# Stacking a head's state and v to 128 stationary rows in a linear-attention and MoE kernel

## The chip, the cores and the metric

The kernel runs on one core of a Trainium2 chip. The metric is the time of one execution on the device, in microseconds. Three executions of the kernel before took 352.67, 353.18 and 351.98 us: a median of 352.67 us.

A core has five engines with an instruction line of their own: PE (TensorE: matmuls, whose weight loads the profile shows as PEld), DVE (VectorE), ACT (ScalarE), POOL (GpSimd) and SP (SyncE, which here issues the DMAs). Each works through its line in the order in which the program wrote it, and waits at an instruction whose inputs are not there yet.

## The reference

```python
def _attn_ref(r, k, v, w, u):              # 4 batches, 8 heads, 768 tokens, 48 dims a head, f32
    for t in range(S):
        kt, vt, rt = (k[:, :, t], v[:, :, t], r[:, :, t])
        cur = np.einsum('bhd,bhe->bhde', u[None] * kt, vt)
        y[:, :, t] = np.einsum('bhd,bhde->bhe', rt, state + cur)
        state = w[None, :, :, None] * state + np.einsum('bhd,bhe->bhde', kt, vt)

def _moe_ref(x, w_in, w_spatial, b_spatial, w_out):   # x: y, heads side by side, (4, 768, 384)
    h = np.maximum(x @ w_in, 0.0)                     # 384 -> 1024
    u, v = (h[..., :d_ff // 2], h[..., d_ff // 2:])
    v_n = (v - mean(v)) / np.sqrt(var(v) + 1e-06)
    v_s = np.einsum('ts,bsd->btd', w_spatial, v_n) + b_spatial[None, :, None]
    return (u * v_s) @ w_out                          # 512 -> 384
```

A linear attention with a decaying state of 48 x 48 a head comes first, and its output y is the input x of a gated MoE block with a spatial matmul over the 768 tokens.

## The kernel before

The tokens of each of the 4 batches are cut into 6 chunks of 128, so there are 24 chunks `m`; `c = m % 6` is the chunk's place in its batch. A chunk is done in two halves of 64 tokens (`z`), and the 8 heads in 4 pairs (`p`). For each chunk stand, in this order of dependence:

- `prep` (L421 to L444): two loads, `rk` (r and k with the dims on partitions) and `rkv` (r, k and v with the tokens on partitions). r and k are scaled by powers of the decay (by DVE and POOL), and POOL builds the tile `a`, whose diagonal is the u term.
- `scores` (L455, called S below): 16 matmuls of 64 x 64 into the PSUM tile `ps`. `products` (L471, P): 16 matmuls k^T v into the same tile, 8 in a batch's last chunk. Both use PE as four tiles of 64 x 64.
- `state` (L485 to L502): a predicated copy on DVE puts the masked scores into `a` (L485); DVE adds the products to the state (`t1`, then `s`, L496 to L502); ACT writes the state of both halves into the block tiles `sblk` (L478 and L479).
- `apply` (L516, A): y of the chunk, into the PSUM tile `xp`. For each half, 12 matmuls multiply scaled r by the state block and 12 multiply `a` by v: 48 in a chunk, 36 in the first chunk of a batch, which has no state for `z == 0`. Each has 128 contraction rows, 32 stationary columns and 64 moving columns, and writes 32 of the 128 output rows. `tile_position=(0, 32 * g)` puts it into one of four strips of 32 columns of PE. The 96 outputs of a head pair are three thirds of 32; the strips `g < 3` take third `g` of the pairs 0 to 2, strip 3 takes the three thirds of pair 3.
- `fin` (L550): xp is split into a rounded part and a rest, the tile `x`.

The MoE part multiplies in the rounded format fp32r three times over (high by high, high by low, low by high: L556, L557, L558), with 384 or 512 moving columns: `moe_v`, `moe_u`, `moe_sp`, `moe_out`. The weights w_in and w_out come as f64 and are taken apart on DVE, ACT and PE (L355 to L378) in the first part of the run; w_sp is split too (`ws_h`, `ws_l`).

The order of every engine's instructions is made when the program is built, by the planner `Plan`: each task has one or more `ways` (an engine, a cost), the planner runs a list schedule over them with its own costs and due times, and the instructions are written in that order. `BIAS` adds to the end time that the planner sees for an engine, so that it chooses another where there is a choice. `SLOTS` gives the number of buffers of each tile; `ps` and `xp` have one each.

Of the kernel before, what the change touches and what calls it, by code (L numbers as in the profile page):

```python
# [7 lines left out]
F32 = mybir.dt.float32  # L8
# [23 lines left out]
OK, OV = DM, DM + DM + 16  # L32
VB = 2 * D
ROW = OV + 2 * NP * VB
# [3 lines left out]
BIAS = 3  # L38
MOST_IN, MOST_OUT = 2, 1


class Task:
    def __init__(self, ways, lag, nominal, nbytes):
        self.ways, self.lag, self.nominal, self.nbytes = ways, lag, nominal, nbytes
        self.cost = min(w[1] for w in ways)
        self.before, self.after, self.bufs = set(), set(), []
        self.due = self.end = self.most = None
# [20 lines left out]
class Plan:  # L68
# [11 lines left out]
    def add(self, ways, r=(), w=(), lag=0.1, nominal=None, nbytes=0):  # L80
        t = Task(ways, lag, nominal, nbytes)
# [46 lines left out]

    def run(self):
# [6 lines left out]
        while ready:  # L136
            best = {}
            for t in ready:
# [4 lines left out]
                if t.nbytes and len(landed) >= self.LANES:  # L143
                    can = max(can, landed[-self.LANES])
                end, e, at = min((max(can, free.get(e, 1.0)) + c + (BIAS if e == "DVE" else 0), e, max(can, free.get(e, 1.0)))
                                 for e, c, *_ in t.ways)
                late = at <= free.get(e, 1.0) + 0.02
                key = (0, t.due, t.place) if late else (1, at, t.due, t.place)
                if e not in best or key < best[e][0]:
                    best[e] = (key, at, t)  # L150
            if not best:
                raise ValueError(f"no slot for any of {len(ready)} ready tasks")
            _, at, t, e = min(((x[0], x[1], x[2], e) for e, x in best.items()), key=lambda x: (x[1], x[2].due))
# [4 lines left out]
            _, cost, emit, two = next(w for w in t.ways if w[0] == e)  # L158
            if two and e == "DVE":
                cost += sum(max(0.0, min(y, at + cost) - max(x, at)) for x, y in shared[-3:])  # L160
            if two and e == "POOL":
                shared.append((at, at + cost))
# [6 lines left out]
            if t.nbytes:  # L169
                line = max(line, at + 1.2)  # L170
                slow = min(t.nbytes / self.SLOW, max(0.0, 5.2 - line))
                line += slow + (t.nbytes - slow * self.SLOW) / self.RATE
                t.end = line + self.FIRST_BYTE
# [11 lines left out]
            emit()  # L185
# [4 lines left out]
def fused_kernel(ctx, tc, rkT, rkvN, wT, uB, w_in, w_sp, b_sp, w_out, out):  # L190
# [4 lines left out]
    EARLY, STATS = 7, 1  # L195
# [3 lines left out]
    SLOTS = dict(rk=3, rkv=3, vn=6, gt=5, u=8, vs=4, g=2, ob=2, pm=4, ps=1, xp=1, x=2, s=2, t1=1, dg=2, q=2)  # L199
# [42 lines left out]
    def load(key, shape, dtype, src, nbytes, view=None, due=None):  # L242
# [3 lines left out]
        plan.add([("SP", 0.45, f, False)], (), [key], lag=0, nbytes=nbytes).most = due  # L246
# [586 lines left out]
```

## Time and profile before

| what | value |
|---|---|
| median of three executions | 352.67 us |
| profiled execution | 352.11 us |
| its span | 350.4 us |
| instructions in the span | 11537 |
| PE busy | 329.4 us |
| DVE, ACT, POOL busy | 171.2, 148.6, 225.3 us |
| apply (L516), from its first matmul to the scores after it, a chunk with a state (at 94.91 us) | 1.48 us |
| HBM read and written | 39.32 MB, 4.72 MB |

The span runs from the first to the last instruction of the core; the execution's own time is longer by what lies around it. In the page's rows a group has its line, engine, operation, `out<-in` by the program's tile names, shapes and count, then busy time, mean duration, and the idle time just ahead of it with what ended it. Rows in order of time begin with the start and the duration in microseconds. A plain f32 matmul leaves two records in the trace, an fp32r matmul one. The granted clock of TensorE was 1.00 in this execution.

### The profile page before, as it was taken

The numbers are of one execution on the slowest core, as the hardware profiler recorded it, in microseconds if no ns is written. First come the engines' busy times: TensorE is split into PE (matmuls) and PEld (weight loads), VectorE is DVE, ScalarE is ACT, GpSimd is POOL, SyncE is SP. The second block draws the span as 40 slices with busy tenths as digits, with TensorE's granted clock in tenths as the row PEclk, the third lists the DMA queues.
The fourth block names the chain that finished last, engine by engine and source line by source line (L and its number), as shares of the span: only waits on it lengthen the run. The fifth ranks groups of instructions, "written<-read, shape, count | busy, mean of one in ns | idle before, by whom it ended". The sixth has DMA issues, their size and how long they took to land.

```text
span 350.4 us, 11537 instructions
## 1 busy us (share of the span) xinstructions
PE 329.4 (94%) x5092; PEld 302.1 (86%) x5092; DVE 171.2 (49%) x353; ACT 148.6 (42%) x334; POOL 225.3 (64%) x215
## 2 busy tenths in 40 slices
PE   2876999899999999999999999999999999999994
PEld 1454678799999899999999899999999899999993
DVE  5598964878634555554233664454233343011030
ACT  4237867772333384641323374640323363611121
POOL 4888989999858765587855767486855240436310
PEclk9999999999999999999999999999999999999999
DMA  7999457762061344442153144342050000010101
GB/s 236 421 408 341 160 177 249 250 227 89 0 199 44 134 153 153 146 129 101 22 199 115 40 152 153 144 137 96 19 203 2 2 2 2 22 47 0 45 24 67
DMA packets 13153, 44.78 MB, mean 128 GB/s; under 512 B 1584, under 2 KB 4784, under 8 KB 13104
## 3 DMA queue, kind: packets, MB, share of 16 engines
q1 hardware_dynamic: 13104, 44.05, 35.4%
q8 instruction: 40, 0.66, 0.8%
q14 instruction: 9, 0.07, 0.1%
HBM read 39.32 MB, written 4.72 MB: 126 GB/s over the span
## 4 chain that ended last, share of the span: by engine, by line
PE 88%; DVE 6%; DMA 2%; issue 2%; ACT 1%; SPq 0%; DVEq 0%; ACTq 0%
PE pm L556 24%; PE pm L557 23%; PE pm L558 23%; PE xp L516 9%; PE ps L455 4%; PE ps L471 3%; DMA vn<-w_in 1%; PE pm L367 1%; DVE a L485 1%; DVE pm L355 1%; DVE vn L357 1%; DVE pm L359 1%; DVE rk L430 1%; DMA out<-ob 1%; DVE wi_l L378 1%
## 5 line engine op out<-in xcount | busy, mean ns | idle before, releaser
L556 PE MATMUL pm<-ws_h,vn 128*128 128x384 f32 x192 | 65.2, 340 | 0.0
L558 PE MATMUL pm<-ws_h,vn 128*128 128x384 f32 x192 | 64.7, 337 | 0.0
L557 PE MATMUL pm<-ws_l,vn 128*128 128x384 f32 x192 | 64.5, 336 | 0.0
L682 DVE TENSOR_TENSOR g<-pm,bb 128x384 f32<-128x384 f32 x32 | 17.8, 556 | 66.6 <-PE pm L558 62.7
L437 POOL TENSOR_TENSOR rkv<-rkv 128x384 f32<-128x384 f32 x24 | 26.3, 1096 | 37.2 <-DMA rkv<-rkvN 37.2
L229 POOL TENSOR_TENSOR vn<-vs,vn 128x512 fp32r<-128x512 f32 x24 | 32.6, 1378 | 27.2 <-ACT vn L233 14.8
L233 ACT CAST gt<-g 128x384 fp32r<-128x384 f32 x32 | 16.4, 514 | 72.6 <-POOL g L229 66.4
L229 POOL TENSOR_TENSOR g<-g,u 128x384 f32<-128x384 f32 x30 | 31.4, 1047 | 19.1 <-DVE g L682 19.1
L434 DVE TENSOR_TENSOR rk<-rk,tt 128x1024 f32<-128x1024 f32 x17 | 29.5, 1734 | 25.9 <-DMA rk<-rkT 25.9
L229 POOL TENSOR_TENSOR gt<-g,gt 128x384 fp32r<-128x384 f32 x30 | 30.5, 1016 | 15.0 <-ACT gt L233 15.0
L556 PEld LDWEIGHTS pm<-ws_h,vn 128*128 128x128 f32 x192 | 36.0, 188 | 0.3
L557 PEld LDWEIGHTS pm<-ws_l,vn 128*128 128x128 f32 x192 | 36.1, 188 | 0.0
L558 PEld LDWEIGHTS pm<-ws_h,vn 128*128 128x128 f32 x192 | 36.0, 188 | 0.0
L556 PE MATMUL pm<-wo_h,gt 128*128 128x384 f32 x96 | 32.9, 342 | 0.0
L556 PE MATMUL pm<-x,wi_h 128*128 128x384 f32 x93 | 32.5, 349 | 0.0
L558 PE MATMUL pm<-wo_h,gt 128*128 128x384 f32 x96 | 32.4, 338 | 0.0
L557 PE MATMUL pm<-wo_l,gt 128*128 128x384 f32 x96 | 32.4, 338 | 0.0
L557 PE MATMUL pm<-x,wi_h 128*128 128x384 f32 x93 | 31.4, 338 | 0.9 <-issue 0.9
L442 POOL TENSOR_TENSOR a<-diag,dg 128x512 f32<-128x512 f32 x24 | 26.1, 1086 | 8.2 <-PE xp L516 4.9
L558 PE MATMUL pm<-x,wi_l 128*128 128x384 f32 x93 | 31.3, 337 | 0.0
L485 DVE COPY_PREDICATED a<-mask,ps 128x512 f32<-128x512 uint32 x24 | 18.0, 751 | 25.8 <-PE ps L471 22.5
L441 POOL TENSOR_TENSOR rkv<-rkv,tn 128x384 f32<-128x384 f32 x24 | 30.2, 1260 | 0.0
(119 smaller groups left out, 701.4 us busy)
## 6 DMA issues: line engine op xcount, KB each, us to landing
rkv<-rkvN SPq DMA_DIRECT2D x24, 776.0 KB, 4.6
rk<-rkT SPq DMA_DIRECT2D x24, 512.0 KB, 6.0
out<-ob SPq DMA_DIRECT2D x24, 192.0 KB, 1.9
vn<-w_in SPq DMA_DIRECT2D x6, 512.0 KB, 10.2
gt<-w_sp SPq DMA_DIRECT2D x6, 384.0 KB, 10.5
gt<-w_out SPq DMA_DIRECT2D x4, 384.0 KB, 3.8
bb<-b_sp SPq DMA_DIRECT2D x1, 384.0 KB, 9.3
ub<-uB SPq DMA_DIRECT2D x1, 192.0 KB, 7.3
```

The costliest lines, as they stand in the source:

```text
L229: plan.add([(e, cost[e], lambda e=e: engine[e].tensor_tensor(**f()), True) for e in ways.split()], r, w)
L233: emit = dict(DVE=lambda: nc.vector.tensor_copy(**f()), ACT=lambda: nc.scalar.copy(f()["out"], f()["in_"]))
L434: dve(1024, lambda: nc.vector.tensor_tensor(out=rk(), in0=rk(), in1=tt.unsqueeze(1).to_broadcast([P, 2, NP, C]), op=ALU.mult), [RK, *TT], ...
L437: pool(DM, lambda: nc.gpsimd.tensor_tensor(out=n_(), in0=n_(), in1=k0(), op=ALU.mult), [RV], [rn])
L441: pool(DM, lambda: nc.gpsimd.tensor_tensor(out=k0(), in0=k0(), in1=tn_f, op=ALU.mult), [RV, rn, *TN], [kn])
L442: pool(512, lambda: nc.gpsimd.tensor_tensor(out=a.rearrange("s b q z t -> s (b q z) t"), in0=diag.unsqueeze(1).to_broadcast([P, H, HC]), i ...
L485: dve(512, lambda: nc.vector.copy_predicated(out=atiles[m % 2].rearrange("s b q z t -> s (b q) (z t)"), mask=mask_u.rearrange("s z t -> s ...
L516: nc.tensor.matmul(xp[32 * g:32 * g + 32, z, jt * HC:(jt + 1) * HC], lhsT, rhs, start=(z, g) not in began, stop=True, skip_group_check=Tru ...
L556: nc.tensor.matmul(o, lh, rh, start=first, stop=False)
L557: nc.tensor.matmul(o, lh, rl, start=False, stop=False)
L558: nc.tensor.matmul(o, ll, rh, start=False, stop=last)
L682: dve(384, lambda: nc.vector.tensor_tensor(out=g(), in0=T[PM][:, 0:TH], in1=bb[:, ts_], op=ALU.add), [PM, ("c", "bb")], [G])
```

## The change

Each head's state and v now stand on top of each other in one tile `sv` of 128 stationary rows (a head's state on the 64 rows of one half of the partitions, its v on the other half), and its scaled r and `a` in one tile `A` of 128 moving rows. So one matmul adds r by state and a by v, for one head `h` of the pair. A third of a pair's outputs that lies within one head takes one matmul, the third that straddles both takes two (`if k != 2 - 2 * h` leaves out the others): 32 a chunk, at a batch's first chunk as well, where the state rows are set to zero.

With it go: v is loaded apart from r and k, by two DMAs into `sv`; the rows of r and a that belong on other partitions are moved by `move`, which the planner gives to SP (a DMA from SBUF to SBUF) or to ACT (a copy); the state is written by four ACT copies instead of two; products takes 48 stationary columns instead of 64; the planner has a bias against ACT too; and `ps` becomes a fixed tile. The MoE part's own work is the same.

```diff
-BIAS = 3
+BIAS = dict(DVE=3.0, ACT=3.5)
...
+    sv = [const.tile([P, 2, 2, NP, HC], F32, name=f"sv{n}") for n in range(NV)]
+    pst = psum.tile([P, 2, 512], F32, name="ps")
...
-        load(("rkv", m), [P, ROW], F32, rkvN[b, c], P * ROW * 4)
+        load(("rkv", m), [P, ROW], F32, rkN[b, c], P * ROW * 4)
+        for h in range(2):
+            sync(sv[m % NV][64 * h:64 * h + 64, h], vN[b, c, h], ("V", m % NV, h), 64 * 2 * NP * HC * 4)
...
+        move(RK + ("r",), ("A", m), "r", [(64 * (1 - t), t, slice(2 * b, 2 * b + 2), 64 * (t ^ b))
+                                          for b in range(2) for t in range(2)],
+             lambda p, h: rk()[h:h + 64, 0, p])
+
+    def move(src, dst, part, places, source):
+
+        for o, t, p, h in places:
+            n = (p.stop - p.start) * C
+            out = lambda o=o, t=t, p=p: tile_of(dst, [P, 2, NP, C])[o:o + 64, t, p]
+            plan.add([("SP", 0.45, lambda out=out, p=p, h=h: nc.sync.dma_start(out=out(), in_=source(p, h)), False, 64 * n * 4),
+                      ("ACT", (n + 220) / 1200, lambda out=out, p=p, h=h: nc.scalar.copy(out(), source(p, h)))],
+                     [src], [dst + ((part, t, p.start),)], lag=0.1)
...
-                nc.tensor.matmul(ps[64 * j:64 * j + 64, b, o:o + D], kn[hs, kc:kc + 64],
-                                 v[hs, z, p, j * D:(j + 1) * D], start=True, stop=True, skip_group_check=True)
...
+                nc.tensor.matmul(ps[64 * j:64 * j + D, b, o:o + D], kn[hs, kc:kc + D],
+                                 sv[m % NV][hs, h, z, p, 16 * h:16 * h + D], start=True, stop=True,
+                                 skip_group_check=True)
...
-        nc.scalar.copy(d4[0:64, :, :, 0:D], src[0:64])
-        nc.scalar.copy(d4[64:P, :, :, D:2 * D], src[64:P])
+    def block(n, z, src):
+        for b in range(2):
+            for j in range(2):
+                h = j ^ b
+                o = 64 * (1 - h)
+                nc.scalar.copy(sv[n][o:o + D, h, z, 2 * b:2 * b + 2, 16 * h:16 * h + D], src[64 * j:64 * j + D, b])
...
+        move(("a", m), ("A", m), "a", [(64 * h, h, slice(0, NP), 64 * h) for h in range(2)],
+             lambda p, h: T["a", m][h:h + 64].rearrange("s b q z t -> s (b q) (z t)"))
...
-            quads = [(jt, g, *((jt, g) if g < 3 else (3, jt))) for jt in range(NK) for g in range(4)]
             for z, s0, t0 in SUBS:
-                if z == 0 and c == 0:
-                    continue
-                for jt, g, p, k in quads:
-                    mm(z, g, jt, sblk[z][:, p, 32 * k:32 * k + 32], rk[:, 0, p, t0:t0 + 64])
-            for z in range(2):
-                for jt, g, p, k in quads:
-                    mm(z, g, jt, v[:, z, p, 32 * k:32 * k + 32], atiles[m % 2][:, p // 2, p % 2, z, :])
-
-        pe(1.55 if c else 1.2, f, [("B", 1), *([("B", 0)] if c else []), ("A", m % 2), ("rk", m, "r"), ("rkv", m)],
-           [XP], nominal=(2 * m + 2, 0))
+                for jt in range(NK):
+                    for g in range(4):
+                        p, k = (jt, g) if g < 3 else (3, jt)
+                        for h in range(2):
+                            if k != 2 - 2 * h:
+                                nc.tensor.matmul(xp[32 * g:32 * g + 32, z, jt * HC:(jt + 1) * HC],
+                                                 sv[n][:, h, z, p, 32 * (k - h):32 * (k - h) + 32],
+                                                 right[:, h, p, t0:t0 + 64], start=(z, g) not in began, stop=True,
+                                                 skip_group_check=True, tile_position=(0, 32 * g))
+                                began.add((z, g))
+
+        pe(1.0, f, [("S", n, 0), ("S", n, 1), ("V", n, 0), ("V", n, 1),
+                    *(("A", m, ("a", h, 0)) for h in range(2)),
+                    *(("A", m, ("r", t, 2 * b)) for b in range(2) for t in range(2))], [XP], nominal=(2 * m + 2, 0))
```

How the order of instructions moves is shown at three places. First PE's line in the steady part, where an apply stands between MoE matmuls (`xp` is apply's PSUM tile, `ps` that of scores and products, `pm` a PSUM tile of the MoE part; `sb` is a state block). Before:

```order
L558 MATMUL pm<-wo_h,gt 128x384
L516 MATMUL xp<-rk,sb_83 32x64 x12
L516 MATMUL xp<-rk,sb_84 32x64 x12
L516 MATMUL xp<-a_82,rkv 32x64 x24
L455 MATMUL ps<-rk 64x64 x16
L471 MATMUL ps<-rkv 64x48 x16
L556 MATMUL pm<-ws_h,vn 128x384
```

and now:

```order
L593 MATMUL pm<-wo_h,gt 128x384
L559 MATMUL xp<-A,sv_82 32x64 x32
L487 MATMUL ps<-rk 64x64 x16
L502 MATMUL ps<-sv_81,rkv 48x48 x16
L591 MATMUL pm<-ws_h,vn 128x384
```

Apply, scores and products stay together, with the same neighbours; only apply's count and the products' shape are others. From there on the stretches of MoE matmuls between two such places are 36, 45, 72, 90 or 99 long in both programs.

Second, SP's line in the steady part, where the loads of later chunks (`rkv`, `rk`) and the stores of results (`out`) stand. Before:

```order
L245 DMA rkv<-rkvN 128x1552
L245 DMA rk<-rkT 128x1024
L702 DMA out<-ob 128x384 x3
L245 DMA rkv<-rkvN 128x1552
L245 DMA rk<-rkT 128x1024
```

and now:

```order
L259 DMA rkv<-rkN 128x768
L259 DMA rk<-rkT 128x1024
L737 DMA out<-ob 128x384 x3
L290 DMA sv_82<-vN 64x512 x2
L474 DMA A<-rk 64x256
L474 DMA A<-a 64x512 x2
L259 DMA rkv<-rkN 128x768
L259 DMA rk<-rkT 128x1024
```

The moves of a chunk (`A`) stand behind stores and v's loads, and ahead of the loads of a later chunk. Over the program SP issues 221 DMAs instead of 93.

Third, DVE's line in the first part, around the fourth chunk's predicated copy and the addition `t<-s,ps` behind it. Before:

```order
L355 TENSOR_SCALAR pm<-vn 128x512
L378 TENSOR_TENSOR wi_l<-pm,wi_h 128x512
L550 TENSOR_TENSOR x<-xp,x 128x2x3x64
L357 SCALAR_TENSOR_TENSOR vn<-vn,pm 128x512
L359 TENSOR_SCALAR pm<-vn 128x512
L430 TENSOR_TENSOR rk<-rk,pm 128x512
L374 SCALAR_TENSOR_TENSOR pm<-vn,pm 128x512
L485 COPY_PREDICATED a_82<-mask,ps 128x512
L496 TENSOR_TENSOR t_638<-s,ps 128x192
```

and now:

```order
L247 CAST ws_h<-gt 128x384
L520 COPY_PREDICATED a<-mask,ps 128x512
L398 TENSOR_TENSOR wi_l<-pm,wi_h 128x512
L450 TENSOR_TENSOR rk<-rk,pm 128x512
L375 TENSOR_SCALAR pm<-vn 128x512
L247 CAST ws_h<-gt 128x384
L377 SCALAR_TENSOR_TENSOR vn<-vn,pm 128x512
L247 CAST x<-xp 128x2x3x64
L379 TENSOR_SCALAR pm<-vn 128x512
L585 TENSOR_TENSOR x<-xp,x 128x2x3x64
L536 TENSOR_TENSOR t_643<-s,ps 128x192
```

Casts of `x` and `ws_h` that ACT did before are now on DVE, here three of them. Over the program DVE has 471 instructions instead of 355, ACT 360 instead of 324, POOL 227 instead of 220.

More of the change, by code (lines that the diff above doesn't have):

```diff
@@ L142, in run @@
                 can = max([1.0] + [b.end for b in t.before] + [min(self.slots[k[0]])[0] for k in takes])
[L143 to L146, printed above, removed]
+                found = None
+                for way in t.ways:
+                    e = way.engine
+                    at = max(can, free.get(e, 1.0))
+                    if way.nbytes and len(landed) >= self.LANES:
+                        at = max(at, landed[-self.LANES])
+                    end = (self.landing(line, at, way.nbytes) if way.nbytes else at + way.cost) + BIAS.get(e, 0.0)
+                    if found is None or end < found[0]:
+                        found = (end, e, at, way)
+                _, e, at, way = found
                 late = at <= free.get(e, 1.0) + 0.02
@@ L157, in run @@
                 s.remove(min(s))
-            _, cost, emit, two = next(w for w in t.ways if w[0] == e)
-            if two and e == "DVE":
+            cost = way.cost
+            if way.two and e == "DVE":
                 cost += sum(max(0.0, min(y, at + cost) - max(x, at)) for x, y in shared[-3:])
-            if two and e == "POOL":
+            if way.two and e == "POOL":
                 shared.append((at, at + cost))
@@ L168, in run @@
             t.end = at + cost + t.lag
[L169 to L173, printed above, removed]
+            if way.nbytes:
+                t.end = self.landing(line, at, way.nbytes)
+                line = t.end - self.FIRST_BYTE
                 landed.append(t.end)
@@ L184, in run, with fused_kernel @@
                     ready.append(a)
-            emit()
+            way.emit()
         assert all(t.end is not None for t in self.tasks)
 @with_exitstack
-def fused_kernel(ctx, tc, rkT, rkvN, wT, uB, w_in, w_sp, b_sp, w_out, out):
+def fused_kernel(ctx, tc, rkT, rkN, vN, wT, uB, w_in, w_sp, b_sp, w_out, out):
     nc = tc.nc
@@ L315, in setup @@
         pool(0, masks, (), [("c", "mask")], cost=1.2)
[L316 to L317 removed]
+        for n in range(NV):
+            for h in range(2):
+                plan.add([("POOL", 0.6, lambda n=n, h=h: nc.gpsimd.memset(sv[n][64 * h:64 * h + 64, 1 - h], 0.0), True),
+                          ("DVE", 0.35, lambda n=n, h=h: nc.vector.memset(sv[n][64 * h:64 * h + 64, 1 - h], 0.0), True)],
+                         (), [("S", n, 0), ("S", n, 1)])
+        dve(0, lambda: nc.vector.memset(pst[:, :, 256:448], 0.0), (), [("c", "pz")], cost=0.5)
         for b in range(2):
@@ L739, in fused_kernel @@
         convert_in(k)
-    for n in range(2):
-        pool(0, lambda n=n: nc.gpsimd.memset(atiles[n], 0.0), (), [("A", n)], cost=0.52)
     for j in range(NS):
```

114 lines of the change are left out of this document (55 added, 59 removed).

## The prediction

> **What bounds the kernel now.** I read the busy shares first, then the sums by stage, then the matmuls in order of time. From the page, the busy row of PE and its forty slices:
>
> ```profile
> PE 329.4 (94%) x5092; PEld 302.1 (86%) x5092; DVE 171.2 (49%) x353; ACT 148.6 (42%) x334; POOL 225.3 (64%) x215
> PE   2876999899999999999999999999999999999994
> ```
>
> and the sums by stage (window; then PE, PEld, DVE, ACT, POOL busy, each with its instructions; clock, DMA share, GB/s):
>
> ```profile
> 0.00:20.00 20.00, 10.40 (x177) 6.57 (x177) 12.40 (x23) 7.65 (x16) 13.20 (x26) 1.00 0.90 339
> 20.00:40.00 20.00, 16.07 (x413) 11.58 (x414) 18.59 (x37) 13.51 (x35) 18.04 (x18) 1.00 0.92 343
> 60.00:80.00 20.00, 18.84 (x381) 16.72 (x373) 15.99 (x38) 15.35 (x40) 20.00 (x18) 1.00 0.72 238
> 80.00:120.00 40.00, 40.00 (x513) 38.47 (x512) 21.70 (x39) 11.07 (x25) 30.90 (x29) 1.00 0.27 93
> 120.00:200.00 80.00, 80.00 (x1320) 74.87 (x1322) 39.61 (x78) 32.91 (x71) 55.37 (x49) 1.00 0.34 116
> ```
>
> There are two regimes. Up to about 45 us PE has holes, and DVE (18.59 of 20), POOL (18.04) and DMA (0.92) are all nearly full: the ramp. From 80 us on PE is never idle, so there a microsecond counts only if it is a microsecond of PE. The chain of waits agrees:
>
> ```profile
> PE pm L556 24%; PE pm L557 23%; PE pm L558 23%; PE xp L516 9%; PE ps L455 4%; PE ps L471 3%; DMA vn<-w_in 1%; PE pm L367 1%; DVE a L485 1%; DVE pm L355 1%; DVE vn L357 1%; DVE pm L359 1%; DVE rk L430 1%; DMA out<-ob 1%; DVE wi_l L378 1%
> ```
>
> The change works on L516 (apply) and L471 (products). Two chunks of the steady stage, as PE sees them (start, duration; the first has a state from before, the second opens a batch and has 36 matmuls instead of 48):
>
> ```profile
> 94.91 0.88 PE L516 MATMUL xp<-rk,sb 128*32 128x64 f32 x48
> 96.39 0.69 PE L455 MATMUL ps<-rk 64*64 64x64 f32 x32
> ...
> 65.11 0.54 PE L516 MATMUL xp<-rk,sb 128*32 128x64 f32 x24
> 66.25 0.69 PE L455 MATMUL ps<-rk 64*64 64x64 f32 x32
> ```
>
> A matmul leaves two records, so 48 matmuls are 96. Apply takes 96.39 - 94.91 = 1.48 us, and 1.14 us at the head of a batch; 12 matmuls are worth 0.34 us, 28 ns each. The question is whether those 28 ns are a price per matmul, or a quarter of what a matmul holds its strip (the 32 columns of PE, and 32 output rows, that `tile_position=(0, 32 * g)` selects). The records of L516 in windows of one step (records in flight in brackets), and how long each lasts:
>
> ```profile
> L516 PE MATMUL xp<-rk,sb x1056: 219/219/243, 17.0 to 290.1; 128*32 128x64 f32 x176
> ...
> 153.16:153.24 0.08, 0.07 (x4) 0.07 (x8) 1.00 0.01 0
> 153.24:153.30 0.06, 0.06 (x8) 0.06 (x12) 1.00 0.00 0
> 153.30:153.35 0.06, 0.06 (x12) 0.06 (x12) 1.00 0.00 0
> 153.35:153.41 0.06, 0.06 (x16) 0.06 (x12) 1.00 0.00 0
> ```
>
> Four records start together every 56 ns, one per strip. And a strip cannot go faster: what streaming costs is seen in full-width matmuls of 512 columns, in the steady stage (L556 to L557), and, in the slower ramp, for plain f32 (L367, two records) beside the rounded format (L368):
>
> ```profile
> 118.16 0.40 PE L556 MATMUL pm<-wi_h,x 128*128 128x512 f32 x1
> 118.39 0.39 PE L557 MATMUL pm<-wi_l,x 128*128 128x512 f32 x1
> ...
> 12.59 1.71 PE pm L367 x2
> 14.30 0.43 PE pm L368
> ```
>
> Start to start 0.23 us for 512 columns is 0.45 ns a column, and plain f32 costs four times as much (1.71 against 0.43 us). So an f32 matmul of 64 columns streams for about 4 x 64 x 0.45 = 115 ns, two steps of 56 ns. Twelve matmuls in each of four strips are 24 steps, 1.34 us, and 0.14 us of switching to the next shape: the 1.48 us. Strips are also not in step: a later group's record starts (27.72) ahead of three of an earlier group (27.76), each strip working off its own line.
>
> ```profile
> 27.72 0.22 PE L516 MATMUL xp<-a,rkv 128*32 128x64 f32 x1
> 27.76 0.23 PE L516 MATMUL xp<-rk,sb 128*32 128x64 f32 x3
> ```
>
> **The change part by part.** *Apply, a chunk with a state.* 32 matmuls instead of 48, but count them by strip. In the new loop `k` is the third of a head pair's 96 outputs; a matmul is left out where `k == 2 - 2 * h`, so thirds 0 and 2 cost one matmul and the middle third, which straddles both heads, costs two. Strip `g < 3` takes `k = g` of pairs 0 to 2, strip 3 takes the three thirds of pair 3. For both `z`: strip 0 has 2 x 3 = 6, strip 1 has 2 x 6 = 12, strip 2 has 6, strip 3 has 2 x 4 = 8. The sum is 32, yet strip 1 keeps its 12, so 24 steps and 1.48 us: gain 0. Were strips served strictly in program order, strip 1's twelve would still follow one another. The upper bound of the gain is the price per matmul, 16 x 28 ns = 0.45 us; I take 0, because 115 ns of streaming does not shrink when other strips are empty. That S (scores) starts early in strips 2 and 3 buys nothing: its other half needs strip 1.
>
> *Apply at the head of a batch.* It had 9 per strip, 18 steps; now it also computes the half with no state, and strip 1 has 12. It takes 1.48 instead of 1.14 us: +0.34 us. Three such chunks (m = 6, 12, 18) lie in the steady stage: +1.0 us.
>
> *Products.* Still 16, but 48 stationary columns instead of 64. The records of L471:
>
> ```profile
> 155.20:155.26 0.06, 0.06 (x8) 0.06 (x12) 1.00 0.31 106
> 155.26:155.32 0.06, 0.06 (x12) 0.06 (x13) 1.00 0.10 27
> ```
>
> The steps are 58 ns, though only 48 columns stream (2 x 48 x 0.45 = 43 ns); 64 columns of weights set them. With 48 columns I take 45 ns: 13 ns over six steps, 0.08 us a chunk, and 0.03 us where only 8 matmuls stand. Fifteen and three such chunks from m = 6 on: -1.3 us (bounds 0 and -1.7, the latter if all 24 count).
>
> *What feeds apply.* r and a must now reach other partitions: 39 r and 41 a DMAs on SP, 57 and 7 copies on ACT, over 24 chunks. In the steady stage the room is the time between products and the next apply. The shortest, over 36 matmuls:
>
> ```profile
> 112.24 0.63 PE L471 MATMUL ps<-rkv 64*64 64x48 f32 x32
> 112.94 0.75 DVE L485 COPY_PREDICATED a<-mask,ps 128x512 f32<-128x512 uint32 x1 [1.96 <-PE ps L471]
> 120.34 0.88 PE L516 MATMUL xp<-rk,sb 128*32 128x64 f32 x48
> ...
> rk<-rkT SPq DMA_DIRECT2D x24, 512.0 KB, 6.0
> out<-ob SPq DMA_DIRECT2D x24, 192.0 KB, 1.9
> ...
> 154.82 0.34 SPq L245 DMA_DIRECT2D rkv<-rkvN  x1
> ```
>
> The predicated copy ends at 113.69; two issues at 0.34 us (the last row) and a landing of 1.9 us, as the 192 KB store has, end at 116.3, four microseconds early. Nor does the wait in SP's queue hurt by itself: behind an a-move stand the loads of a chunk further on. The four small state copies (two before) lie in the same room. Cost 0 while that cover holds; without it, the second rival.
>
> *The ramp.* Here other engines decide. Where the fourth apply waits today:
>
> ```profile
> 37.22 0.55 DVE L550 TENSOR_TENSOR x<-xp,x 128x384 fp32r<-128x384 f32 x1
> 37.68 0.68 DVE L357 SCALAR_TENSOR_TENSOR vn<-vn,pm 128x512 uint32<-128x512 uint32 x1
> 40.83 0.33 DVE L496 TENSOR_TENSOR t<-s,ps 128x192 f32<-128x192 f32 x1
> 41.19 0.35 ACT L478 COPY sb<-t 64x192 f32<-64x192 f32 x1 [1.33 <-DVE t L496]
> 41.60 0.85 PE L516 MATMUL xp<-rk,sb 128*32 128x64 f32 x21 [0.44 <-ACT sb L478]
> ...
> L596 ACT ACTIVATE q<-q 128x1 f32<-128x1 f32 x6 | 1.2, 205 | 0.1
> ...
> 14.47 0.69 DVE L355 TENSOR_SCALAR pm<-vn 128x512 uint32<-128x512 uint32 x1 [1.75 <-DMA vn<-w_in]
> ```
>
> DVE adds t, ACT copies it, PE starts: DVE is first. By the order of instructions, five casts that ACT did (three of x, two of ws_h) now stand on DVE ahead of that addition; one of 384 columns takes 0.46 us of its line (37.22 to 37.68), so +2.3 us. ACT makes four copies of 96 columns instead of two of 192; between 0.20 us for one column (L596) and 0.35 for 192 I take 0.27, so 1.1 instead of 0.7: +0.4 us. On the other side loads get lighter: 1552 columns become 768, with v's 512 apart and later, so 0.54 MB fewer lie ahead of the third w_in, for which DVE waited at 14.47; at the stage's 0.34 to 0.41 MB/us that is -1.3 us or more. Together +1.4 us at the fourth apply. Later holes in PE's line can swallow some of it:
>
> ```profile
> 61.96 0.45 PE L557 MATMUL pm<-x,wi_h 128*128 128x384 f32 x1 [0.85 <-issue]
> 67.39 0.56 PE L471 MATMUL ps<-rkv 64*64 64x48 f32 x23 [0.31 <-issue]
> ```
>
> I let half arrive: +0.7 us. Bounds: -1.3 (only the loads count) and +4 (DVE has nine added instructions by its last conversion of w_in, some 3.6 us, plus ACT's 0.4, nothing swallowed).
>
> **Sum:** 0 + 1.0 - 1.3 + 0.7 = +0.4 us. The profiled execution took 352.11 us (350.4 of span and 1.7 around it), 0.56 below the median of the three, 352.67; so the median should come to 353.1 us.
>
> **Rivals.** *First: the price is per matmul.* Then apply falls by 16 x 28 ns = 0.45 us in the 17 chunks with a state from m = 4 on, 4 x 28 ns in three: -7.7 - 0.3; with products and the ramp -8.6, 344.1 us. For it: 28 ns fits both readings of the trace before, since its strips were all equally loaded. Against it: four starts every 56 ns, and the streaming of 115 ns per matmul. [...]
>
> *Second, slower: the moves come late.* The route from products to a landed a has 120.34 - 112.24 = 8.1 us over 36 matmuls, and about 10 us over the nine stretches of 45 (7.54 x 45 / 36 + 0.56 = 10.0). It takes 4 us by the store's 1.9, and 8.1 if moves land like the 6.0 us loads: the point from which it decides. At 10.5 us, with a store ahead in SP's line waiting for its result, PE loses 2.4 + 9 x 0.5 = 7 us: 360 us. For it: moves, stores and loads share one line in order. Against: DMA is at 0.27 to 0.34 there.
>
> *Third, slower: DVE or POOL bound the ramp,* at the upper bound of that term: 4 instead of 0.7, 356.4 us. For it: POOL is busy 20.00 of 20 us from 60 to 80, and DVE gets 116 more instructions. *Fourth, the lighter loads win:* the ramp at -1.3 gives 351.1 us, and more if each ramp chunk profits.
>
> **How the numbers follow.** The forecast, with its own range of 351 to 355.5, gets 0.55; the first rival 0.14, the second 0.13, the third 0.12, the fourth 0.06. A measurement of this kernel tells 0.3% (1.06 us) from no change. The forecast's 0.55 splits into 0.08 faster, 0.30 same, 0.17 slower. Faster: 0.08 + 0.14 + 0.06 = 0.28; same 0.30; slower 0.17 + 0.13 + 0.12 = 0.42. The range leaves out the first rival and half of the second: 349 to 360.5 us.
>
> **What would show it.** Right: apply still 1.48 us to the next scores, at heads of batches too, with four records starting together in the first steps and one alone at the end; products at 45 ns a step; PE without holes after 80 us. The first rival: apply at about 1.0 us. The second: idle time ahead of the apply line, released by a DMA or by ACT's copies of A. The third: PE reaching its closed line later than 46 us. The forecast is wrong if strip 1's records come faster than one in 56 ns, or if PE shows holes after 80 us.

## The result and the profile after

The changed kernel takes 362.29 us (median of 4, 361.72 to 363.30), the kernel before beside it 352.50 us (351.98 to 353.18). The ratio is 1.028, with a 95% interval of 1.0249 to 1.0310: 9.8 us slower. The forecast was 353.1 us, its range ended at 360.5. The profiled execution took 363.30 us, with a span of 361.4 us. Of one kernel below (balanced strips with `BIAS` without ACT) two of the four executions lay more than 1.5% above its fastest, and only its other two are compared.

The page of the changed kernel: busy shares, PE and its granted clock in forty slices, and the chain of waits by engine.

```profile
PE 332.7 (92%) x4420; PEld 303.6 (84%) x4420; DVE 230.5 (64%) x469; ACT 134.0 (37%) x370; POOL 226.7 (63%) x222
PE   2793897899999999999999999999999999999994
PEclk9988799989999999999999999999999999999999
PE 72%; DMA 16%; DVE 6%; POOL 2%; issue 1%; SPq 1%; DVEq 0%; ACT 0%; POOLq 0%
```

DMA now holds 16% of the chain (58 us, of which some 42 lie ahead of 90 us), and the granted clock, which was 1.00 in every window shown of before, has low slices, all of them ahead of 81 us. So both point at the ramp, by which from here on everything ahead of some 87 us is meant. The sums by stage of the changed kernel (columns as before: window, PE, PEld, DVE, ACT, POOL, clock, DMA share, GB/s):

```profile
0.00:20.00 20.00, 10.45 (x148) 6.30 (x149) 14.68 (x28) 10.36 (x24) 14.30 (x27) 1.00 0.91 292
20.00:40.00 20.00, 13.39 (x273) 9.99 (x265) 16.63 (x33) 15.83 (x45) 14.80 (x15) 0.76 0.99 338
60.00:80.00 20.00, 15.60 (x299) 13.81 (x300) 13.56 (x28) 12.16 (x38) 18.51 (x19) 0.91 0.62 182
80.00:120.00 40.00, 39.60 (x457) 38.05 (x457) 32.93 (x62) 15.55 (x41) 34.81 (x32) 1.00 0.50 153
120.00:200.00 80.00, 79.14 (x1197) 73.69 (x1200) 49.07 (x102) 28.70 (x81) 53.09 (x49) 1.00 0.47 137
```

From 20 to 40 us DVE and POOL are busy *less* than before (16.63 and 14.80 us instead of 18.59 and 18.04). The ramp did not get longer because these engines were full; they waited. The ninth apply (m = 8) starts at 104.7 us instead of 94.9, +9.8 us. From there to the last apply it is 195.9 instead of 194.6 us, and the 306 matmuls behind that take as long as before. So all but about one microsecond was lost ahead of the steady stage. Half of it was lost by the fourth apply, which starts at 46.30 us (before, its part with a state at 41.60: +4.7 us), the other half between there and the ninth.

In the steady stage the PE line reads as the prediction has it. Two chunks of the changed kernel (the second opens a batch):

```profile
104.70 1.53 PE L559 MATMUL xp<-A,sv 128*32 128x64 f32 x64
106.16 0.69 PE L487 MATMUL ps<-rk 64*64 64x64 f32 x32
106.68 0.54 PE L502 MATMUL ps<-sv,rkv 64*48 64x48 f32 x32
...
152.69 1.53 PE L559 MATMUL xp<-A,sv 128*32 128x64 f32 x64
154.16 0.69 PE L487 MATMUL ps<-rk 64*64 64x64 f32 x32
```

Apply with 32 matmuls takes 1.46 us to the next scores, where 48 took 1.48; at the head of a batch it takes 1.47 where it took 1.14.

In the ramp, these are the three longest holes of the changed kernel's PE behind 10 us, and what follows them (PEld, DVE: the rows of these engines that bear on the first two; the last row is DVE's wait for the third w_in, at 14.47 us before):

```profile
32.36 0.89 PE L502 MATMUL ps<-sv,rkv 64*48 64x48 f32 x32 [2.01 <-issue]
32.68 0.45 PEld L502 LDWEIGHTS ps<-sv,rkv 64*48 64x48 f32 x30 [0.19 <-DMA sv<-vN]
36.18 0.34 DVE L542 TENSOR_TENSOR s<-ps,w 128x192 f32<-128x192 f32 x1
36.62 1.13 PE L487 MATMUL ps<-rk 64*64 64x64 f32 x32 [3.38 <-POOL rkv L458]
...
39.13 0.63 PE L591 MATMUL pm<-wi_h,x 128*128 128x512 f32 x1
39.56 0.63 PE L592 MATMUL pm<-wi_l,x 128*128 128x512 f32 x1
...
40.40 0.40 PE L591 MATMUL pm<-wi_h,x 128*128 128x512 f32 x1
40.63 0.39 PE L592 MATMUL pm<-wi_l,x 128*128 128x512 f32 x1
...
73.09 1.85 PE L559 MATMUL xp<-A,sv 128*32 128x64 f32 x64 [2.39 <-DMA A<-a]
...
13.98 0.69 DVE L375 TENSOR_SCALAR pm<-vn 128x512 uint32<-128x512 uint32 x1 [1.83 <-DMA vn<-w_in]
```

The products at 32.36 us are those of the third chunk; by the semaphore counts of the trace (each transfer raises its semaphore sixteen times; the last count is its landing) the second half of their v landed at 32.6 us, having been issued at 24.4, and the PEld row shows the wait for it. Before, v came with r and k and that load had landed at 17.5 us. Behind the products the state update on DVE runs late, until 36.52 us, and the next scores wait 3.38 us for it, since there is one ps buffer. (The row names POOL's `rkv`, which ended at the same moment and which scores do not read; the wait that PE's line holds there is for DVE's semaphore.) And how fast does the full DMA line move its bytes? The kernel before and the changed one:

```profile
10.00:20.00 10.00, 8.27 (x145) 4.73 (x144) 5.97 (x11) 3.60 (x7) 8.92 (x9) 1.00 1.03 419
20.00:30.00 10.00, 7.41 (x172) 4.75 (x172) 9.83 (x20) 4.26 (x10) 8.99 (x9) 1.00 1.02 404
```
```profile
10.00:20.00 10.00, 7.23 (x115) 3.97 (x114) 7.03 (x13) 5.65 (x14) 8.66 (x9) 0.99 1.04 342
20.00:30.00 10.00, 8.84 (x197) 6.40 (x191) 9.11 (x19) 8.43 (x24) 8.40 (x9) 0.83 1.04 375
```

The DMA engines are busy all the time in both (share 1.02 to 1.04), yet move 342 instead of 419 GB/s from 10 to 20 us.

### The profile page after: what moved, and what is told of

The parts are those of the page before. It is cut to its first block, busy times and chain, and to the rows that moved or that the text cites. A ratio compares the mean times of both kernels' runs of the same rounds, so it can differ in the third digit from the quotient of the medians.

```text
span 361.4 us, 10654 instructions
## 1 busy us (share of the span) xinstructions
PE 332.7 (92%) x4420; PEld 303.6 (84%) x4420; DVE 230.5 (64%) x469; ACT 134.0 (37%) x370; POOL 226.7 (63%) x222
## 4 chain that ended last, share of the span: by engine, by line
PE 72%; DMA 16%; DVE 6%; POOL 2%; issue 1%; SPq 1%; DVEq 0%; ACT 0%; POOLq 0%
PE pm L591 20%; PE pm L593 20%; PE pm L592 19%; PE xp L559 8%; DMA rk<-rkT 6%; DMA rkv<-rkN 5%; PE ps L487 3%; DMA A<-a 3%; PE ps L502 2%; DMA vn<-w_in 1%; DVE rk L454 1%; DVE q L639 1%; POOL gt L243 1%; DVE a L520 1%; DVE x L247 1%
## 5 line engine op out<-in xcount | busy, mean ns | idle before, releaser
L454 DVE TENSOR_TENSOR rk<-rk,tt 128x1024 f32<-128x1024 f32 x17 | 28.1, 1656 | 33.4 <-DMA rk<-rkT 30.4
L243 POOL TENSOR_TENSOR vn<-vs,vn 128x512 fp32r<-128x512 f32 x24 | 31.2, 1316 | 24.3 <-DVE vn L247 14.7
L559 PEld LDWEIGHTS xp<-A,sv 128*32 128x32 f32 x1536 | 33.8, 109 | 13.3 <-issue 5.1
L243 POOL TENSOR_TENSOR g<-g,u 128x384 f32<-128x384 f32 x30 | 30.4, 1012 | 22.4 <-DVE g L717 22.4
L559 PE MATMUL xp<-A,sv 128*32 128x64 f32 x1536 | 38.3, 227 | 6.3 <-DMA A<-a 3.7
L462 POOL TENSOR_TENSOR a<-diag,dg 128x512 f32<-128x512 f32 x24 | 27.3, 1137 | 26.2 <-DMA A<-a 24.6
L475 ACT COPY A<-rk 64x256 f32<-64x256 f32 x57 | 23.0, 404 | 47.6 <-PE xp L559 34.5
L591 PE MATMUL pm<-x,wi_h 128*128 128x384 f32 x93 | 32.6, 351 | 0.0
## 6 DMA issues: line engine op xcount, KB each, us to landing
gt<-w_sp SPq DMA_DIRECT2D x6, 384.0 KB, 10.1
```

The source lines that it names most:

```text
L243: plan.add([(e, cost[e], lambda e=e: engine[e].tensor_tensor(**f()), True) for e in ways.split()], r, w)
L454: dve(1024, lambda: nc.vector.tensor_tensor(out=rk(), in0=rk(), in1=tt.unsqueeze(1).to_broadcast([P, 2, NP, C]), op=ALU.mult), [RK, *TT], ...
L462: pool(512, lambda: nc.gpsimd.tensor_tensor(out=a().rearrange("s b q z t -> s (b q z) t"), in0=diag.unsqueeze(1).to_broadcast([P, H, HC]), ...
L475: ("ACT", (n + 220) / 1200, lambda out=out, p=p, h=h: nc.scalar.copy(out(), source(p, h)))],
L559: nc.tensor.matmul(xp[32 * g:32 * g + 32, z, jt * HC:(jt + 1) * HC], sv[n][:, h, z, p, 32 * (k - h):32 * (k - h) + 32], right[:, h, p, t0: ...
L591: nc.tensor.matmul(o, lh, rh, start=first, stop=False)
```

## The experiments

Five theories for the ramp. **P** (not the products): a transfer that writes 64 rows runs at half the rate, and the change loads v in two of these. **C**: it is the number and size of transfers. **V**: the load of v waits in SP's line for the apply two chunks before. **M**: the moves of a queue behind loads. **B**: the ACT entry of `BIAS` puts casts on DVE. **O** came later: PE's order. (D, in the expectations of the loads apart, is 'loads apart slow the full line'; it was split into P and C afterwards.) Beside them it is tested whether the fullest strip sets the time of apply. An edit that changes a cost or a dependence lets the planner make another order of the instructions; where every engine's order stayed the same, the text says so. The kernel before took 351.9 to 352.9 us beside each group of runs; differences below about 1 us are not told apart.

**Balanced strips** (changed kernel; w_in's rows are permuted to match):

```
-                        p, k = (jt, g) if g < 3 else (3, jt)
+                        p, k = g, jt
```

> Edit on the changed kernel: strip g takes the three thirds of pair g (p, k = g, jt), the rows of w_in are permuted to match; still 32 matmuls, but 8 in every strip instead of 6, 12, 6, 8. The order of all engines is the same. Theory 'the fullest strip sets it': 16 steps of 56 ns instead of 24, apply 1.46 - 0.45 = about 1.0 us to the next shape; the 16 or so applies behind the ramp alone give -7 us, all 24 give -11: between 351 and 355 us. Rival 'price per matmul' (the 32 cost what they cost because they are 32): apply stays 1.46 us and the time 362.3. Second rival: apply shortens but PE then waits for the moves, and the time falls by less than 4 us.

359.80 us (357.51 to 361.90). PE's line, with the order of all engines unchanged:

```profile
102.33 1.16 PE L559 MATMUL xp<-A,sv 128*32 128x64 f32 x64
103.41 0.69 PE L487 MATMUL ps<-rk 64*64 64x64 f32 x32
```

The same 32 matmuls take 1.08 instead of 1.46 us once no strip has more than 8: eight steps less, 47 ns each. So here the fullest strip set the time of apply. But of 0.38 us x 16 = 6 us in the steady stage nothing arrives: m = 8 to the last apply is 195.6 us, as without the edit (195.9), and the 2.5 us that the kernel gained came ahead of m = 8 (102.33 instead of 104.70). Eight holes of 4.1 us in sum opened behind 86 us; PE's waits there:

```profile
PE pm L593 <- POOL gt L243: 1.3, 3, 0.5
PE pm L591 <- DVE gt L247: 0.9, 1, 0.9
PE pm L593 <- DVE x L585: 0.9, 2, 0.5
```

**All moves on ACT** (changed kernel):

```
-            plan.add([("SP", 0.45, lambda ...: nc.sync.dma_start(out=out(), in_=source(p, h)), False, 64 * n * 4),
-                      ("ACT", (n + 220) / 1200, lambda ...: nc.scalar.copy(out(), source(p, h)))],
+            plan.add([("ACT", (n + 220) / 1200, lambda ...: nc.scalar.copy(out(), source(p, h)))],
```

> Edit on the changed kernel: all moves of r and a are copies on ACT, none is a DMA on SP (80 DMAs less, 80 copies more, about 41 us more of ACT over the kernel). Theory M 'the moves queue behind the loads in the DMA line': the four holes ahead of apply that end with the landing of an a-move (3.7 us of PE, and what follows from them) go, the 99-matmul stretch of the steady stage starts 4 to 5 us earlier (about 82 instead of 86.7 us) and the time is 357 to 358.5. Theory V 'the v loads come late': the hole of the products of the third chunk (32.4 us) and the one behind it stay, and the time stays within 1.5 us of 362.3. If the moves also hold up the v loads by taking places in SP's line: 353 to 355. Rival: ACT becomes the bound of the ramp, over 363.

371.45 us (370.06 to 371.68). The rival: no PE hole ends with a move's landing any more, but PE waits for ACT and for the DVE work behind it (from 46 to 130 us):

```profile
PE ps L486 <- DVE s L541: 6.1, 2, 5.7
PE xp L558 <- ACT A L474: 3.7, 3, 2.6
```

It could not judge M, since it replaced one late engine by another.

**v loaded apart, in the kernel before.** The load of r, k and v is cut into one of r and k and two of v with 64 rows each, with three buffers for v:

```
-        load(("rkv", m), [P, ROW], F32, rkvN[b, c], P * ROW * 4)
+        load(("rkv", m), [P, OV], F32, rkvN[b, c, :, 0:OV], P * OV * 4)
+        for h in range(2):
+            load(("vv", m, h), [P, ROW - OV], F32, rkvN[b, c, 64 * h:64 * h + 64, OV:ROW], ...)
```

> Edit on the kernel before: v is loaded apart from r and k, in two DMAs of 64 rows, as the change does, into a tile of its own with three buffers; nothing else. Theory D 'more and smaller transfers make the full DMA slower': the bytes moved from 10 to 20 us fall from 419 towards 342 GB/s and the ramp grows, +2 to +5 us (355 to 357.5). Theory V (below, the wait) and theory M (the moves): within 1 us of 352.5.

and with `vv=2` buffers, so that the load waits for the apply two chunks before:

> As the kernel before with v loaded apart in two DMAs, but with two buffers for v, as the change has: a load of v now waits in SP's line for the apply two chunks before. Theory V 'this wait, in SP's line ahead of other loads, is what the ramp pays for': +3 to +6 us over the one with three buffers. Theory D: the same as with three buffers (within 1 us). Theory M: both as the kernel before, 352.5.

368.75 us (365.84 to 370.21) with three buffers, 357.24 us (357.08 to 360.35) with two. In the kernel before V does not hold: with the wait it is the faster one. But the two have different orders, so the 11.5 us between them are not the price of a buffer, and no run gave the changed kernel a third buffer. There SP's line does stand still for the apply two chunks before, 10.4 us in four waits from 10 to 90 us; with v in 128 rows (below) it is 22.2 us in nine waits, and that version is the faster one. The same bytes with v in two 64-row transfers cost the kernel before 17 us in the one order and 5 in the other, where D had expected 2 to 5. To part P from C, the two transfers of v are cut by columns, with packets of half the length:

```
-            load(("vv", m, h), ..., rkvN[b, c, 64 * h:64 * h + 64, OV:ROW], ..., lambda t, h=h: t[64 * h:64 * h + 64])
+            load(("vv", m, h), ..., rkvN[b, c, :, OV + 384 * h:OV + 384 * h + 384], ..., lambda t, h=h: t[:, 384 * h:384 * h + 384])
```

> Edit on the kernel before with v apart and three buffers (368.75 us): the two DMAs of v are cut by columns (128 rows x 384 columns each) instead of by rows (64 rows x 768 columns); count, bytes and the order on all engines are the same. Theory P 'a transfer to 64 rows runs at half the rate': the bytes moved from 10 to 20 us go from 302 back to about 400 GB/s and most of the 17 us go: 352 to 358. Theory C 'count and packet size': with packets of half the length it stays at 366 to 372.

359.63 us (358.64 to 360.31). The DMA line full, cut by rows and then by columns:

```profile
10.00:20.00 10.00, 7.09 (x144) 3.93 (x144) 6.97 (x13) 3.63 (x7) 8.31 (x9) 0.98 1.03 302
20.00:30.00 10.00, 7.46 (x153) 4.97 (x157) 6.56 (x16) 1.99 (x5) 7.14 (x7) 0.85 1.04 337
```
```profile
10.00:20.00 10.00, 7.90 (x144) 4.49 (x144) 6.78 (x12) 3.63 (x7) 8.57 (x9) 1.00 1.04 409
20.00:30.00 10.00, 7.79 (x205) 5.32 (x205) 8.77 (x19) 3.88 (x10) 10.00 (x11) 1.00 1.03 408
```

Same bytes, count and order on every engine: 302 against 409 GB/s, and 9.1 us (10.1, each against the kernel before beside it). P is shown for the rate. The time stays 7 us above the kernel before, and above the 352 to 358 expected: three loads in another order of SP's line have a price of their own, which no run took apart.

**The same in the changed kernel.** v as two transfers of 128 rows instead of 64, the order of all engines unchanged (it leaves out the right placing of v, so only its time counts; the lines shown leave out that the zeroing of the tile is fitted to it):

```
-            sync(sv[m % NV][64 * h:64 * h + 64, h], vN[b, c, h], ("V", m % NV, h), 64 * 2 * NP * HC * 4)
+            sync(sv[m % NV][:, 0, h], vN[b, c].rearrange("h s z p e -> (h s) z p e")[:, h], ("V", m % NV, h), ...)
```

> Edit on the changed kernel: the two DMAs of v write 128 rows x 256 columns each instead of 64 rows x 512 columns; same count, bytes and order on every engine. It leaves the right placing of v out (the second head half is not loaded, one half of the tile holds both), so its output is not the reference's; only its time counts. Theory P 'a transfer to 64 rows runs at half the rate': with 128 rows the pair takes 0.65 instead of 1.1 to 1.5 us of a full DMA line, the v of the third chunk lands 3 to 4 us earlier than 32.6 us, and the time falls by 2 to 6 us (356 to 360). Theory C 'the number of transfers and the places they take in SP's line': within 1 us of 362.3. Theory M 'the moves come late': within 1.5 us of 362.3.

356.49 us (355.84 to 357.15): 5.8 us of the 9.8 (6.2, each against the kernel before beside it).

```profile
10.00:20.00 10.00, 7.35 (x138) 4.25 (x137) 8.26 (x16) 7.23 (x18) 10.00 (x11) 1.00 1.03 403
20.00:30.00 10.00, 6.98 (x204) 5.31 (x202) 8.68 (x18) 6.55 (x20) 8.14 (x8) 1.00 1.04 406
```

By the semaphore counts (from the first count of one transfer to the first of the next) the third chunk's pair of v takes 0.69 us of the full line instead of 1.16, the transfer behind it no longer takes 0.4 us more than its kind, and v is there at 29.1 instead of 32.6 us. The hole ahead of the next scores is as long as it was (3.39 us), but opens 3.6 us earlier: its length is that of the state update, which stands between products and scores whenever v comes. The fourth apply starts at 43.14 us, 1.5 instead of 4.7 us later than in the kernel before; by m = 8 the 1.5 have become 4.3.

**BIAS without ACT** (changed kernel), alone and with balanced strips:

```
-BIAS = dict(DVE=3.0, ACT=3.5)
+BIAS = dict(DVE=3.0)
```

> Edit on the changed kernel: BIAS has no ACT entry, as before the change, so the planner gives the casts back to ACT (331 instead of 448 rows on DVE, 259 instead of 174 on ACT), and 51 moves of r and a go to SP instead of 80. Theory B 'the casts on DVE make the ramp late': 354 to 358 us. Theory P 'the v loads set it': the start of the steady stage moves by less than 2 us, 360 to 364 us. Rival: ACT is then late with the moves, over 364.

> The changed kernel with both edits: strips balanced (8 matmuls in each) and BIAS without ACT. With strips balanced alone, eight holes of 4.1 us in sum opened behind 86 us, most of them ended by casts and subtractions of x on DVE, and ate the 6 us that the shorter applies gave. If these waits come from the casts that the ACT entry puts on DVE, they close and the kernel gains the whole 0.38 us x 24 = 9 us on the one with BIAS alone (8 +- 2 us under it). If not, it gains no more than 3 us on it, as balancing alone did.

382.29 us (381.33 to 382.93), and 371.44 and 376.10 us (two executions, in the order of the first). The casts go back to ACT, which has the moves and four state copies where it had two, and is busy 217.9 us; PE then waits for the state chain (first row: the busy row; second: the longest of PE's waits):

```profile
PE 340.8 (89%) x4420; PEld 310.2 (81%) x4420; DVE 169.8 (45%) x354; ACT 217.9 (57%) x539; POOL 222.1 (58%) x222
...
PE ps L487 <- DVE s L542: 7.8, 2, 5.9
```

So the entry is not a slip: with the moves on ACT, the changed kernel needs it, and what the casts cost its ramp cannot be read by taking it out. Balancing gains between 6 and 11 us on it: the expected 8 fits, but two executions so far apart do not show it.

**Only a on ACT** (r keeps both ways), the same with v in 128 rows, and with balanced strips:

```
-                      ("ACT", (n + 220) / 1200, lambda ...: nc.scalar.copy(out(), source(p, h)))],
+                      ("ACT", (n + 220) / 1200, lambda ...: nc.scalar.copy(out(), source(p, h)))][part == "a":],
```

> Edit on the changed kernel: the moves of a (the ones that apply waits for) are copies on ACT only; r keeps both ways. 41 DMAs less on SP, 41 copies of 0.62 us more on ACT over the kernel, and no r copy less. Theory M 'a moves queue behind loads': the holes of PE ahead of apply that end with a landing of A<-a (0.4 at 55, 0.9 at 62, 2.4 at 70.7, with the clock lost behind them) go, 3 to 4 us: 358 to 359.5. If they are only cover for another late input: 361 to 364. Rival: ACT is late with a, as when it made all moves: over 365.

> Both edits on the changed kernel: v in two DMAs of 128 rows (output not the reference's, alone 356.5 us) and a by ACT only, in the order of the one with a by ACT alone. If half-rate v loads and queued a moves together are the whole of the 9.7 us: 352 to 354. If something third remains in the ramp (casts on DVE, ACT copies): 355 to 357.

> Both edits on the changed kernel: balanced strips (8 matmuls in each, alone 359.8 us) and a by ACT only. If both gains are independent: 355 to 357. If the shorter apply only moves the waits, within 1 us of the one with a by ACT alone.

With a on ACT: 362.47 us (362.17 to 362.75), no change; with v in 128 rows too, in the same order: 356.58 us (356.41 to 359.06), the same as without a on ACT, and 5.9 us less for the rows alone. The holes that ended with a landing of a did go, and others of like length came, in DVE's line:

```profile
61.27 1.01 PE L487 MATMUL ps<-rk 64*64 64x64 f32 x32 [3.53 <-DVE t L536]
...
70.53 1.74 PE L559 MATMUL xp<-A,sv 128*32 128x64 f32 x64 [2.46 <-DVE x L585]
```

The late moves are not the price, then, though the planner's order is another here. With balanced strips and a on ACT: 355.04 us (354.27 to 355.97), 7.4 us under the one without balancing, in the same order: here most of the gain arrives (m = 8 to the last apply in 188.4 instead of 193.5 us, the rest in the ramp). It is the fastest version that computes the reference's output, and 0.9% slower than the kernel before (ratio 1.0088, 1.0061 to 1.0115).

**The planner told the price of 64 rows** (changed kernel; the same for `move`):

```
-            sync(..., ("V", m % NV, h), 64 * 2 * NP * HC * 4)
+            sync(..., ("V", m % NV, h), 2 * 64 * 2 * NP * HC * 4)
```

> Edit on the changed kernel: the planner is told that v loads and moves, which write 64 rows, take twice the line time (bytes counted twice in its table); the program has the same operations in another order, with 48 moves more or less on either side. Theory P (64 rows, half the rate) says that the order was planned on a wrong price: 354 to 360. Rival: order does not matter, the bytes do: 361 to 364.

365.72 us (364.22 to 365.84), slower: neither the expected gain nor no change. A better price in the table did not make a better order.

**PE's order.** Scores and products of a chunk held behind the apply of the chunk before, as the kernel before has them (the lines shown leave out a line of the planner that lets instructions of PE follow each other without a lag):

```
+        [..., ("ap", m - 1)], [PS + ("s",)], nominal=(2 * m, 1))     # scores; products likewise
+        ..., [XP, ("ap", m)], nominal=(2 * m + 2, 0))                # apply
```

> Edit on the changed kernel: scores and products of a chunk are planned behind the apply of the chunk before (one key more that apply writes and they read; same-engine order without the planner's lag), so PE's line is 'apply, scores, products' everywhere, as in the kernel before; the operations are the same. Theory O 'scores placed ahead of apply stop PE for the state update of the chunk before, since there is one ps buffer': the 3.4 us hole at 33 us goes and 2 to 4 us of it arrive: 358 to 360.5. If the hole is only where the lateness of v shows: 361 to 364.

> The same edit with v in two DMAs of 128 rows (output not the reference's; 356.5 us without the order edit). If order and v loads together are the whole of the 9.7 us: 352 to 354. If the casts on DVE (or something else) hold the rest: 355.5 to 357.5.

> The changed kernel with three edits that keep the output: balanced strips, a by ACT only, and apply ahead of the next scores in PE's line. Without the order edit 355.0 us. Theory O: 351 to 353.5, level with the kernel before or under it. Otherwise 354 to 357.

365.23 us (363.36 to 366.05), 361.32 (359.60 to 362.51) and 355.49 (354.10 to 357.35). The hole of 3.38 us went and time was lost all the same, now ahead of apply (waits of the first from 10 to 110 us):

```profile
PE xp L559 <- ACT A L475: 5.0, 5, 1.7
PE xp L559 <- DMA A<-a: 3.1, 3, 2.3
```

O does not hold: with the scores behind it, PE waits for apply's inputs instead, at least in the order that the planner made of it. From the first to the second, in the same order, the 128 rows gain 3.9 us.

**BIAS with ACT, in the kernel before** (the entry alone):

```
-                end, e, at = min((... + c + (BIAS if e == "DVE" else 0), e, ...)
+                end, e, at = min((... + c + dict(DVE=3.0, ACT=3.5).get(e, 0.0), e, ...)
```

> Edit on the kernel before: BIAS gets the ACT entry of 3.5 (448 rows on DVE instead of 337, 193 on ACT instead of 256), nothing else. Theory B 'the casts on DVE hold the rest of the ramp': 355 to 358 us. Otherwise within 1 us of 352.5; faster is possible too, since the same entry makes the changed kernel 20 us faster.

355.38 us (355.32 to 355.52), +3.1. Until 65 us the applies start within about 1.5 us of the kernel before; then two holes come, in DVE's line, the second of the same kind as with a on ACT above (apply waiting for DVE's subtraction):

```profile
75.25 0.69 PE L455 MATMUL ps<-rk 64*64 64x64 f32 x32 [1.93 <-DVE s L502]
...
81.52 0.88 PE L516 MATMUL xp<-rk,sb 128*32 128x64 f32 x48 [1.79 <-DVE x L550]
```

**v with its zeros in one transfer of 128 rows**, twice the bytes (512 KB a chunk; the instructions that set zeros go, the host lays them out), on the changed kernel and with balanced strips and a on ACT:

```
-        for h in range(2):
-            sync(sv[m % NV][64 * h:64 * h + 64, h], vN[b, c, h], ("V", m % NV, h), 64 * 2 * NP * HC * 4)
+        plan.add([("SP", 0.45, lambda: nc.sync.dma_start(out=sv[n], in_=vN[b, c]), False, P * 4 * NP * HC * 4)], (),
+                 [("V", n, 0), ("V", n, 1), ("S", n, 0), ("S", n, 1)], lag=0)
```

> Edit on the changed kernel: v of a chunk comes with the zeros of the other half as one DMA of 128 rows x 1024 columns, 512 KB instead of two of 128 KB to 64 rows; the memsets of zeros go, the state copies wait for the load; output as the reference's. Theory P: 512 KB at the full rate take 1.28 us of the line, the pair takes 1.1 to 1.5, so twice the bytes cost nothing: 359 to 363 us. Theory 'bytes count': 256 KB more in each of nine ramp chunks at 410 GB/s are 0.62 us each, 365 to 368.

> The same load of v with balanced strips and a by ACT only (355.0 us without the new load). Theory P: 353 to 355.5; level with the kernel before at best, since the ACT entry of BIAS still costs the ramp its 3 us. Theory 'bytes count': 358 to 361.

363.10 us (362.89 to 364.04) and 360.65 us (357.95 to 361.76). On the changed kernel twice the bytes cost less than 1 us, which fits P but, with fewer instructions and another order, does not prove it; the line now moves 410 GB/s from 10 to 20 us, and more of it is zeros. On the balanced version it is 5.6 us slower than the pair, which neither theory had; its order differs, and why it loses stays open.

## Why the prediction was wrong

*The four steady terms were right.* Apply with a state: gain 0 forecast, 0.02 us measured, and for the reason given: balancing the strips shortened the same 32 matmuls by 0.38 us, against 0.45 by eight steps of 56 ns. Head of a batch: +0.34 forecast, 1.47 - 1.14 = +0.33. Products: -0.08 and -0.03 a chunk forecast, 0.56 to 0.47 and 0.33 to 0.29 measured, with 48 stationary columns instead of 64 and 48 moving columns in both. The moves in the steady stage: no hole there ends with a move. Still 1.3 us were lost behind m = 8 where these terms, over the 16 chunks there, give a gain of some 0.8 us. Of these 2.1 us, 1.3 are four holes in which PE waits for DVE's work on x (two subtractions, one cast) and POOL's gt, the rest is lost in the same blocks of matmuls (one of 45 took 9.59 us where it had taken 8.56). I had set nothing for casts there. With a on ACT the same stretch takes 193.5 us, 1.1 less than before: there the gain is seen.

*The ramp term failed.* It said +0.7 us, with bounds of -1.3 and +4; 9.8 were measured, more than twice the upper bound. Two of its parts were mis-sized, and so was the step from the fourth apply to the end:

- "Loads get lighter", -1.3 us. I took bytes over the rate of a full line, 0.34 to 0.41 MB/us, for transfers of a kind that the kernel before does not have. The two loads of v write 64 rows each, and these ran at about half the rate: 256 KB in 1.12 to 1.24 us, and 0.4 us more for the transfer behind them, where two of 128 rows take 0.69 to 0.73. The third w_in, on which the term was worked out, landed at 13.89 us instead of 14.37, 0.5 us earlier; with v in 128 rows it landed at 13.14, 1.2 us earlier, as summed. Over the whole ramp the rows cost +5.8 us by the run that changed them alone, so there the sign was wrong too. In rates, the pair's 256 KB move at 211 to 234 GB/s, about half of the 403 to 409 that the line has with v in 128 rows, although the two transfers of a pair write the two halves of the rows. Why the transfers of 64 rows were slower, no run took apart.
- "Five casts more on DVE", +1.4 with copies, of which I let half arrive. The mechanism was right: alone, in the kernel before, the entry costs 3.1 us. The size was not: the casts do harm as late as 73 to 81 us, in a part of the ramp that I did not look at.
- "I let half arrive." At the fourth apply +1.4 us was forecast and 4.7 measured; with v in 128 rows it was 1.5. But the delay was not swallowed on the way to m = 8, it grew: 4.7 to 9.8, and 1.5 to 4.3. That the 1.5 meet the 1.4 says nothing for the parts of that sum, which no run took one by one.

5.8 + 3.1 = 8.9 of the 9.8 us. The two prices come from two kernels, each with an order of its own (in three orders of the changed kernel the rows alone cost 5.8, 5.9 and 3.9 us), so that they add up is likely, not shown; the rest is open, the wait of v's loads for the apply among it.

*The rivals.* The second (late moves) showed its sign, holes of 0.3 to 2.4 us that end with a landing of a, in the ramp and not in the steady stage; but without them, in another order, the time was the same. The third foresaw the side and the stage, for another reason: DVE and POOL were less busy, not full. The first is out by the balanced strips (32 matmuls, 1.08 us), the fourth by the time.

*The upper bound* was the real fault. It was built from added instructions only; the row of a transfer of 64 rows was missing in the profile of before, and for what a profile does not show, a bound needs more than the cheapest reading.

## What to carry to other kernels

A layout that saves TensorE work may cut a load into transfers of half the rows; price them at half the rate (here 211 to 234 instead of 403 to 409 GB/s, on a full DMA line) until a trace shows otherwise. Where column strips of PE are used, count matmuls by strip: here the fullest one was the time (32 matmuls, 1.46 us with 12 in it, 1.08 us with 8). And a hole in PE's line names the last input, not the cause: three edits took such holes away here and the time stayed or rose (362.47, 365.23 and 371.45 us against 362.29). All three also moved the planner's order, so undo the suspected cause with the order unchanged before believing, or dismissing, it.

## What the runs showed of the hardware

- With the DMA engines busy throughout (share 1.03 and 1.04 from 10 to 20 us), v in 64-row transfers among others of 128 rows brought the line from 409 to 302 GB/s, with the same bytes, number of transfers and order. Packets of half the length did not matter beside that: the version with 409 GB/s has the shorter ones.
- A hole cost PE more than its length. In the changed kernel the granted clock is 0.50 from 33.55 to 40.37 us, over the hole of 3.38 us and behind it, and the 512-column matmuls start 0.43 us apart until about 40.2 us, then 0.23 us. The same stretch of the changed kernel, and of the kernel before, which had no hole there:

```profile
36.60:40.00 3.40, 3.38 (x38) 2.80 (x39) 3.40 (x6) 3.28 (x11) 3.30 (x3) 0.50 0.76 208
```
```profile
36.60:40.00 3.40, 3.40 (x75) 2.66 (x74) 3.37 (x7) 3.18 (x9) 3.40 (x4) 1.00 0.91 331
```

  PE looks as busy in both and does half the matmuls (38 against 75). At half the clock for 3.4 us, 1.7 us of PE's work were lost on top of the hole, by my estimate from these rows. Whether they reach the end of the kernel is not shown: executions of the kernel before with a mean clock of 0.982 and 0.994 took 351.66 and 352.23 us.
- In the changed kernel the granted clock goes from 1.00 to 0.50 or back at 19.89, 23.31, 33.55, 40.37, 74.51 and 77.92 us, all whole multiples of 3.41 us apart. In the 3.41 us ahead of each of these three stretches at 0.50 PE was busy for 1.34, 1.04 and 1.41 us. It was busy for 1.31 us from 6.24 to 9.65 us too, and the clock behind that stayed at 1.00: what sets the clock is not shown.
